# The order of products in the steps of a fused attention and Mish kernel

## Chip, cores and metric

One core of one Trainium2 chip. The metric is the device time of one execution in microseconds, the median of several runs.

## The reference

The input x is 1 x 2048 x 512. It is normalised over its last axis to xn. One branch is attention with 32 query heads of 16 and a single key and value head of 16; the other is a dense layer to 1792, Mish, and a dense layer back to 512. The sigmoid-weighted output of the second branch gates the first, and x is added.

```python
q = (xn @ wq)  as 32 heads of 16;  k = xn @ wk;  v = xn @ wv      # one k, one v for all heads
p = softmax(q k^T * 16**-0.5);  s = concat_heads(p v) @ wo
h = xn @ w1 + b1;  act = h * tanh(softplus(h));  g = silu(act @ w2)
out = x + s * g
```

All arrays are float32. The factors of 8 on the weights make the scores large enough that the softmax needs the row maximum.

## The kernel before

The four heads of a virtual group `v` (32 groups: four chunks of 512 queries times eight groups of heads) are treated together. A group takes 16 steps for its 16 blocks of 128 keys, so the main loop has 512 steps `s`. In each step PE issues:

- Four scores (`e_one`, L875): 128 keys by 512 queries from a contraction of 64 rows, into one of three banks `e`. ACT turns each into its exponential `pt` (L877).
- Four products for the row maxima of a later group (`m_one`, L895): 128 queries by 512 keys, into one of three banks `m`. DVE takes the maximum of each (L899). The maxima go back as extra rows of the queries, so that the exponential needs no bias of its own.
- A chunk of the dense work: the projections of q, the two dense layers and the output projection. A dense group accumulates 9 to 15 products of 128 rows in the only bank `x` (`xps`). `chunk_size` cuts a group of 12 into two chunks of six and one of 15 into chunks of eight and seven. Each product is split into two halves of 64 rows (`Mm.half`, L109): one step issues the lower halves of the chunk, the next the upper halves.
- The product of the exponentials of step s - 2 with the values (`pv`, L949).

Two products of 64 rows can run side by side on the two halves of PE's rows. `waves` writes out the order by hand. In step s the dense halves `xs` stand on side h = s % 2, followed by that side's products for maxima (the queue `b`). On the other side, 1 - h, stands the queue `a`: the four scores and n products for maxima, merged after the pattern `EM`; `m_sides` sets n, half the number of dense halves within limits given by `MLAG`. One round of the loop issues one dense half (or, when they are out, one product of `b`) and then one product of `a`; the last of `a` waits until the halves are out. With six halves n is 3 and `b` has one product, so a step has seven rounds; with seven halves, eight.

The two halves of one bank must not be written at once. `waves` therefore keeps a `relay`: the instruction on ACT or DVE that consumes a product issued after the last dense half of the step. The first dense half of the next step of the same group waits for it. When a group ends, `finish` calls its `post`, which empties the bank on ACT or DVE; for groups emptied by DVE, maxima of the last rounds are held back behind that (`HOLD`). After the products, ACT gets one or two pending jobs (`act_jobs`), and then comes `pv`.

Before the main loop a planner with costs and due times orders the normalisation, the first projections and the first maxima. The last 22 steps (`LEAD`) have no products for maxima, and the last groups of the dense work run unsplit after the loop. The engines' program orders are fixed when the kernel is built; on the chip only waits move them.

Of the kernel before, what the change touches and what calls it, by code (L numbers as in the profile page):

```python
# [41 lines left out]
STEP_US = 2.95  # L42
XMAX = 8
NPT = 14
EM = "MEMEMEME"
MLAG = 4
NHB = 3
NACT = 7
# [11 lines left out]
def m_need(v):  # L60

    return (40, 64)[v] if v < 2 else 32 * (v + 1)
# [53 lines left out]
def block_kernel(ctx: ExitStack, tc: tile.TileContext, x, wq, wk, wv, wo, w1, b1, w2, out):  # L116
# [348 lines left out]
    def begin():  # L465
        prepare()
        if qqueue and is_ready(qqueue[0]):
            g = qqueue.popleft()
        elif queue and is_ready(queue[0]):
            g = queue.popleft()  # L470
        else:
            n = next((n for n, g in enumerate(queue) if g.wo is None), None)
            if not n or not is_ready(queue[n]) or queue[n].m1 is None:
                return False
            g = queue[n]
            del queue[n]
        if g.start:
            g.start()
        if g.alloc:
            ps = g.alloc()  # L480
        else:
            ps = ps_x.tile([P, 512], F32, tag="x", name="xps")
        cur.update(g=g, n=0, ps=ps, chunk=[], relay=None)
        return True

    def finish():
        g = cur["g"]
        if cur["n"] < len(g.mms):
            return False
        for i in g.items:  # L490
            i.users -= 1
        cur["g"] = None
        evacs[0] += g.dve
        if lead:
            lead["post"](g, cur["ps"])
        else:
            g.post(cur["ps"])
            g.done = step[0]
        return True
# [14 lines left out]
    def chunk_size(n):  # L514
        return -(-n // -(-n // XMAX)) if n else 0

    def waves(h, em, new):

        if not cur["chunk"] and (not new or cur["g"] is None and not begin()):
            mms = []
        else:
            g = cur["g"]
            mms = cur["chunk"] or g.mms[cur["n"]:cur["n"] + chunk_size(len(g.mms) - cur["n"])]
        second = bool(cur["chunk"])
        k = len(mms)
        ms = em(k)
        a = deque(ms[1 - h])  # L530
        b = deque(ms[h])
        ps = cur["ps"]
        ends = second and cur["n"] + k == len(cur["g"].mms)
        xs = deque(mms)
        relay = None
        first = True
        done = False
        while a or b or xs:
            if xs:
                i = xs.popleft().half(ps, h)  # L540
                if first and cur["relay"] is not None:
                    tc.add_manual_dep(i.ins, cur["relay"].ins.name, mybir.DependencyInfo(
                        mybir.DependencyClass.Sync, mybir.DependencyReason.DATA), reason="other half of the bank")
                first = False
                if ends and cur["g"].dve and len(xs) == HOLD:
                    held[0] = []
                if not xs and ends:
                    cur["n"] += k
                    cur["chunk"] = []
                    finish()  # L550
                    done = True
                    for top in held[0] or ():
                        top()
                    held[0] = None
            elif b:
                b.popleft()()
            if len(a) > 1 or a and not xs:
                r = a.popleft()()
                if k and not xs and relay is None:
                    relay = r  # L560
        if k and not done:
            assert relay is not None
            cur["relay"] = relay
            if second:
                cur["n"] += k
                cur["chunk"] = []
            else:
                cur["chunk"] = mms
# [295 lines left out]
    def e_one(s, i):  # L864

        v, r = divmod(s, 16)
        if s < NS - LEAD:
            a, k, p = 1 - s % 2, r - r % 2 + i // 2, i % 2
        else:
            a, k, p = i % 2, r, i // 2  # L870
        q = qt_of[v]
        o = 64 * a
        ps, tag = (ps_m, "m") if NS - LEAD <= s and i in ((1, 3) if s < NS - 4 else (3,)) else (ps_e, "e")
        e = ps.tile([P, C], F32, tag=tag, name=f"e{s}_{i}")
        pe.matmul(e, ks[o:o + 64, P * k:P * (k + 1)], q[o:o + 64, p], start=True, stop=True)  # L875
        pt = sb.tile([P, C], F32, tag="pt", name=f"pt{s}_{i}", bufs=NPT)
        r = act.activation(pt, e, AF.Exp, scale=0.25)  # L877
        pt_of[16 * v + k, p, a] = pt
        return r
# [3 lines left out]
    def m_one(a):  # L883
        v, n = MSEQ[m_next[a]] if m_next[a] < 64 else divmod(m_next[a], 32)
        m_next[a] += 1
        if v not in mb_of:
            mb_of[v] = sb.tile([P, 4, 16], F32, tag="mb", name=f"mb{v}", bufs=2)
        q = qt_of[v]
        kb, j = divmod(n, 8)
        p, t = divmod(j, 4)  # L890
        o = 64 * a
        ps, tag = (ps_e, "e") if lead and 15 in xp_of and a else (ps_m, "m")
        m = ps.tile([P, C], F32, tag=tag, name=f"m{v}_{a}_{n}")
        o = slice(o, o + (HALF if v < len(qts) else 48))
        pe.matmul(m, q[o, p, P * t:P * (t + 1)], ks[o, C * kb:C * (kb + 1)], start=True, stop=True)  # L895
        z = 8 * a + 4 * p + t

        def top():
            return dve.reduce_max(out=mb_of[v][:, kb, z:z + 1], in_=m, axis=AX.X)  # L899
        if held[0] is None:  # L900
            return top()
        held[0].append(top)

    def m_sides(h, n):

        ahead = m_next[h] - m_next[1 - h]
        lo = max((4 - MLAG - ahead + 1) // 2, 4 - (32 * NU - m_next[1 - h]))
        hi = min((4 + MLAG - ahead) // 2, 32 * NU - m_next[h])
        return max(min(n, hi), lo)
# [116 lines left out]
    def due(t):  # L1026
        step[0] = t
        for k in sorted(k for k in timed if k <= t):
            for fn in timed.pop(k):
                fn()  # L1030
# [85 lines left out]
    for c0, c1 in ((0, 1), (1, 2), (2, 4)):  # L1116
# [4 lines left out]
        for c in range(c0, c1):  # L1121
            xs, his = [], []
# [29 lines left out]
            if c == 0:  # L1152
                qp = task("PE", 2.8, lambda: fill(12), xs)
                xs = [qp]
# [45 lines left out]
    while True:  # L1200
# [21 lines left out]
        s, e, k = min(opts, key=lambda o: o[0])  # L1222
# [36 lines left out]
        elif k == "J":  # L1259
            tag = next((g for g in ("wq", "ws", "wb") if arrived(g) and busy[0] + E0 < s + 0.5), None)  # L1260
            n = ran[0]
# [16 lines left out]
    while left:  # L1278
        k = next(k for k in left if all(d.end is not None for d in k.deps))
# [6 lines left out]
    for s in range(NS + 2000):  # L1286
        inm = s < NS - LEAD
        if inm or cur["chunk"]:
            assert s < NS
            due(s)  # L1290
            h = s % 2

            def em(k):
                n = m_sides(1 - h, k // 2) if inm else 0
                x = deque(lambda i=i: e_one(s, i) for i in range(4))
                y = deque(lambda: m_one(1 - h) for _ in range(n))
                r = [[], []]
                for op in EM:
                    if op == "M" and y:
                        r[1 - h].append(y.popleft())  # L1300
                    elif op == "E":
                        r[1 - h].append(x.popleft())
                r[h] = [lambda: m_one(h) for _ in range(4 - n if inm else 0)]
                return r

            if s >= 2 and (s - 1) % 16 == 0 and s > 1:
                gap[0] += 1
            waves(h, em, inm)
            act_jobs(1 + (len(jobs) > 2))
            due(s + 0.5)  # L1310
            if s >= 2:
                pv(s - 2)
                if (s - 1) % 16 == 0 and s > 1:
                    o_out((s - 17) // 16)
        else:
            due(s)
            if s < NS:
                for i in range(4):
                    e_one(s, i)
                fill(4)  # L1320
            act_jobs(2 if s < NS else 100)
            if s < NS + 2:
                pv(s - 2)
                if (s - 1) % 16 == 0:
                    o_out((s - 17) // 16)
            due(s + 0.5)
            if s >= NS:
                fill(16)
        step[0] = s
        if vdone[0] < 8 * NC and min(m_next) >= m_need(vdone[0]):  # L1330
            r = c_rows(vdone[0])
            rowq.extend([r[0], r[1], lambda r=r: (r[2](), r[3]())])
            vdone[0] += 1
        if rowq and not evacs[0]:
            rowq.popleft()()
        evacs[0] = 0
        pump()
        if s > NS + 1 and not queue and cur["g"] is None and not timed and not jobs:
            break
# [12 lines left out]
```

## Time and profile before

| What | Value |
|---|---|
| Median of 3 runs | 1616.48 us (1615.63 to 1619.14) |
| Span of the profiled execution, first to last instruction | 1612.9 us |
| PE busy | 1594.2 us, 99% |
| DVE busy | 1348.5 us, 84% |
| ACT busy | 1294.7 us, 80% |
| POOL busy | 620.8 us, 38% |
| Mean granted clock of PE | 0.999 |

The page gives the span of the profiled execution, and no time of its own beside it; the median of the runs is 3.6 us above that span. Engines: PE is the matrix engine, PEld its weight loads, DVE the vector engine, ACT the scalar engine, POOL the general one, SP the engine that issues the DMAs. In a row of the timeline the columns are the start, the duration, the engine, the line, the operation, the tile written and the tiles read, the shapes, and the number of instructions merged; behind that may stand the idle time before it and what ended it. In a row of the list of waits stand the waiting engine and tile, the one waited for, the total, the number of times and the longest.

### The profile page before, as it was taken

How to read it: one execution, taken by the hardware profiler on the slowest of the kernel's cores; microseconds unless marked ns; L12 is line 12 of the kernel's file. 1: busy time of each engine (PE TensorE's matmuls, PEld its weight loads, DVE VectorE, ACT ScalarE, POOL GpSimd, SP SyncE). 2: the span in 40 equal slices, each digit the busy share in tenths (PEclk: the TensorE clock that was granted, in tenths of full speed). 3: DMA queues.
4: the chain of work that ended last, by engine and by line, in shares of the span. 5: the costliest groups of instructions: out<-in, count | busy, mean ns of one | idle time of the engine just before them, and what ended most of it. 6: DMA issues, size and time to landing. Idle time of an engine off the chain costs nothing.

```text
span 1612.9 us, 31471 instructions
## 1 busy us (share of the span) xinstructions
PE 1594.2 (99%) x11615; PEld 851.9 (53%) x11615; DVE 1348.5 (84%) x2300; ACT 1294.7 (80%) x2490; POOL 620.8 (38%) x627
## 2 busy tenths in 40 slices
PE   8999999999999999999999999999999999999998
PEld 5455545555555555555555555555555555555534
DVE  8988888888988888888898988888889898888802
ACT  5478788788888778877988787797788878879885
POOL 3875176166265103421524133154153223315522
PEclk9999999999999999999999999999999999999999
DMA  5332133042231304212113321231241313022020
GB/s 161 145 115 64 41 122 111 15 148 83 70 114 52 109 23 153 70 31 91 52 27 111 92 75 26 91 119 38 67 135 34 113 57 96 23 73 78 21 86 26
DMA packets 72776, 127.30 MB, mean 79 GB/s; under 512 B 21488, under 2 KB 34288, under 8 KB 72112
## 3 DMA queue, kind: packets, MB, share of 16 engines
q1 hardware_dynamic: 72624, 125.30, 24.9%
q8 instruction: 92, 1.51, 0.4%
q14 instruction: 60, 0.49, 0.1%
HBM read 76.36 MB, written 27.26 MB: 64 GB/s over the span
## 4 chain that ended last, share of the span: by engine, by line
PE 95%; DVE 2%; ACT 1%; DMA 1%; issue 0%; POOL 0%; SPq 0%; DVEq 0%; ACTq 0%; POOLq 0%
PE xps L109 46%; PE pv L949 31%; PE m L895 8%; PE e L875 5%; PE xps L105 3%; DVE mb L899 1%; PE wop L105 1%; PE warm L1178 0%; PE kp L289 0%; ACT xin L194 0%; DMA xin<-in_dram 0%; DVE st L214 0%; DMA ws<-w 0%; DVE xin L240 0%; PE xp L250 0%
## 5 line engine op out<-in xcount | busy, mean ns | idle before, releaser
L899 DVE TENSOR_REDUCE mb<-m 128x1 f32<-128x512 f32 x2048 | 1272.8, 683 | 184.4 <-PE m L895 157.5
L877 ACT ACTIVATE pt<-e 128x512 f32<-128x512 f32 x2048 | 1068.4, 604 | 253.0 <-PE e L875 236.8
L895 PE MATMUL m<-ks,qt 48*128 48x512 f32 (+1 forms) x2048 | 837.4, 422 | 3.0 <-DVE mb L899 2.5
L875 PE MATMUL e<-qt,ks 64*128 64x512 f32 x2048 | 746.4, 410 | 0.0
L949 PE MATMUL pv<-pt,vaug 128*32 128x512 f32 x4096 | 545.3, 605 | 0.0
L895 PEld LDWEIGHTS m<-ks,qt 48*128 48x128 f32 (+1 forms) x2048 | 370.6, 185 | 67.2 <-DVE mb L899 35.2
L875 PEld LDWEIGHTS e<-qt,ks 64*128 64x128 f32 x2048 | 370.7, 186 | 26.3 <-ACT pt L877 19.6
L109 PE MATMUL xps<-xt,ws 64*128 64x512 f32 x1248 | 345.8, 410 | 0.4 <-POOL ws L153 0.2
L109 PEld LDWEIGHTS xps<-xt,ws 64*128 64x128 f32 x1248 | 215.2, 185 | 205.9 <-ACT pt L877 135.2
L109 PE MATMUL xps<-wbs,act 64*128 64x512 f32 x1158 | 312.9, 407 | 0.1
L109 PEld LDWEIGHTS xps<-wbs,act 64*128 64x128 f32 x1158 | 201.9, 185 | 166.8 <-ACT pt L877 101.5
L949 PEld LDWEIGHTS pv<-pt,vaug 128*32 128x32 f32 x4096 | 80.7, 108 | 141.9 <-issue 133.2
L163 POOL TENSOR_SCALAR t<-t 128x512 f32<-128x512 f32 x56 | 34.5, 616 | 278.4 <-ACT t L658 278.4
L153 POOL TENSOR_TENSOR hb<-hb,t 128x512 f32<-128x512 f32 x56 | 72.3, 1292 | 152.4 <-PE m L895 74.0
L109 PE MATMUL xps<-xt,wq 64*128 64x512 f32 x336 | 93.0, 409 | 0.0
L109 PEld LDWEIGHTS xps<-xt,wq 64*128 64x128 f32 x336 | 58.0, 185 | 55.4 <-ACT pt L877 35.2
L109 PE MATMUL xps<-wbs,ot_all 64*128 64x512 f32 x288 | 79.3, 407 | 0.0
L109 PEld LDWEIGHTS xps<-wbs,ot_all 64*128 64x128 f32 x288 | 49.5, 184 | 47.2 <-ACT pt L877 30.2
L153 POOL TENSOR_TENSOR hb<-hb,u 128x512 f32<-128x512 f32 x56 | 72.3, 1291 | 4.4
L153 POOL TENSOR_TENSOR u<-u,t 128x512 f32<-128x512 f32 x56 | 71.9, 1284 | 4.7
L153 POOL TENSOR_TENSOR act<-hb,act 128x512 fp32r<-128x512 f32 x55 | 70.9, 1289 | 4.6
L721 DVE TENSOR_TENSOR y<-xps,y 128x512 f32<-128x512 f32 x32 | 21.9, 683 | 58.0 <-PE xps L105 58.0
(116 smaller groups left out, 826.7 us busy)
## 6 DMA issues: line engine op xcount, KB each, us to landing
ws<-w SPq DMA_DIRECT2D x38, 512.0 KB
wbs<-w SPq DMA_DIRECT2D x36, 512.0 KB
qt<-qh SPq DMA_DIRECT2D x256, 32.0 KB
w<-ws SPq DMA_DIRECT2D x14, 512.0 KB
w<-wbs SPq DMA_DIRECT2D x14, 512.0 KB
wq<-wq SPq DMA_DIRECT2D x13, 512.0 KB
wbs<-wo SPq DMA_DIRECT2D x12, 512.0 KB
rawwb<-in_dram SPq DMA_DIRECT2D x20, 256.0 KB
```

Of the source, the lines that this page charges most:

```text
L105: self.pe.matmul(ps, self.lhs(), self.rhs(), start=(self.k == 0), stop=(self.k == self.tot - 1))
L109: i = self.pe.matmul(ps, self.lhs()[o], self.rhs()[o], start=(self.k == 0 and self.halves == 0), stop=(self.k == self.tot - 1 and self.hal ...
L153: eng.tensor_tensor(out=o, in0=a, in1=b, op=op)
L163: pool.tensor_scalar(o, o, lim, 0.0, op0=ALU.min, op1=ALU.max)
L721: dve.tensor_tensor(out=y, in0=ps, in1=y, op=ALU.add)
L875: pe.matmul(e, ks[o:o + 64, P * k:P * (k + 1)], q[o:o + 64, p], start=True, stop=True)
L877: r = act.activation(pt, e, AF.Exp, scale=0.25)
L895: pe.matmul(m, q[o, p, P * t:P * (t + 1)], ks[o, C * kb:C * (kb + 1)], start=True, stop=True)
L899: return dve.reduce_max(out=mb_of[v][:, kb, z:z + 1], in_=m, axis=AX.X)
L949: pe.matmul(o[32 * j:32 * j + 32], vaug[:, k], pt, start=(k == 0), stop=(k == 15))
```

## The change

In a step with fewer than eight dense halves, and some, in which n is 3, the side with the scores takes the pattern E M E M E M E in place of M E M E M E E. The relay becomes the consumer of the last product that is issued after the halves, in place of the first one.

```diff
-EM = "MEMEMEME"
+EM = ("MEMEMEME", "EMEMEME")
...
             if len(a) > 1 or a and not xs:
                 r = a.popleft()()
-                if k and not xs and relay is None:
+                if k and not xs:
                     relay = r
...
-                for op in EM:
+                for op in EM[0 < k < XMAX and n == 3]:
                     if op == "M" and y:
                         r[1 - h].append(y.popleft())
                     elif op == "E":
```

## The prediction

> **What bounds the kernel now.** I read the page first, then the list of waits, then the timeline of single steps, and last the stretches by window.
>
> ```profile
> span 1612.9 us, 31471 instructions
> PE 1594.2 (99%) x11615; PEld 851.9 (53%) x11615; DVE 1348.5 (84%) x2300; ACT 1294.7 (80%) x2490; POOL 620.8 (38%) x627
> ...
> PE 95%; DVE 2%; ACT 1%; DMA 1%; issue 0%; POOL 0%; SPq 0%; DVEq 0%; ACTq 0%; POOLq 0%
> ...
> L899 DVE TENSOR_REDUCE mb<-m 128x1 f32<-128x512 f32 x2048 | 1272.8, 683 | 184.4 <-PE m L895 157.5
> L877 ACT ACTIVATE pt<-e 128x512 f32<-128x512 f32 x2048 | 1068.4, 604 | 253.0 <-PE e L875 236.8
> ```
>
> PE carries 95% of the chain of waits. Its program order is fixed, so the time is the sum of its steps, and a wait inside a step is added directly. Two consumers empty its banks: a maximum takes DVE 683 ns, an exponential takes ACT 604 ns. Here is one undisturbed step with six dense halves (PE and weight loads in the timeline, then the first maximum and the first exponential by themselves):
>
> ```profile
> 808.94 0.16 PEld L949 LDWEIGHTS pv<-pt,vaug 128*32 128x32 f32 x8 [0.25 <-issue]
> ...
> 809.79 0.65 ACT L729 ACTIVATE e<-y 128x512 f32<-128x512 f32 x1
> 809.94 0.18 PEld L109 LDWEIGHTS xps<-wbs,act 64*128 64x128 f32 x1 [0.84 <-ACT pt L877]
> ...
> 809.94 0.50 PE L895 MATMUL m<-ks,qt 48*128 48x512 f32 x1
> ...
> 810.28 0.40 PE L875 MATMUL e<-qt,ks 64*128 64x512 f32 x1
> ...
> 810.51 1.89 DVE L899 TENSOR_REDUCE mb<-m 128x1 f32<-128x512 f32 x3 [0.37 <-PE m L895]
> ...
> 811.22 0.40 PE L875 MATMUL e<-qt,ks 64*128 64x512 f32 x1
> 811.26 0.18 PEld L895 LDWEIGHTS m<-ks,qt 48*128 48x128 f32 x1
> 811.37 0.18 PEld L875 LDWEIGHTS e<-qt,ks 64*128 64x128 f32 x1
> ...
> 811.79 0.16 PEld L949 LDWEIGHTS pv<-pt,vaug 128*32 128x32 f32 x8 [0.24 <-issue]
> ...
> 810.51 0.69 DVE L899 TENSOR_REDUCE mb<-m 128x1 f32<-128x512 f32 x1 [0.37 <-PE m L895]
> ...
> 810.72 0.60 ACT L877 ACTIVATE pt<-e 128x512 f32<-128x512 f32 x1 [0.28 <-PE e L875]
> ```
>
> The step is pv (808.94 to 809.94, 1.00 us) and then seven slots of two matmuls, one on each half of the rows (809.94 to 811.79, 1.85 us). The first slot takes 0.34 us (809.94 to 810.28), because its weight load is bare; the others take some 0.235 us ((811.22 - 810.28)/4). I call the products on the score side M1, E1, M2, E2, M3, E3, E4, with M4 on the other side in the seventh slot just ahead of E4. Both kinds have three banks, so M4 needs the bank of M1, and E4 that of E1. E1 comes a slot later than M1: its exponential ends at 811.32 and E4's load starts at 811.37, 0.05 us after. So E4 is the tight one, and when E1's exponential is late, pv is late by as much:
>
> ```profile
> 744.09 0.60 ACT L877 ACTIVATE pt<-e 128x512 f32<-128x512 f32 x1 [0.65 <-PE m L895]
> ...
> 744.74 0.18 PEld L875 LDWEIGHTS e<-qt,ks 64*128 64x128 f32 x1 [0.28 <-ACT pt L877]
> ...
> 745.17 0.16 PEld L949 LDWEIGHTS pv<-pt,vaug 128*32 128x32 f32 x8 [0.24 <-issue]
> ...
> PEld xps L109 <- ACT pt L877: 302.1, 360, 1.1
> PEld m L895 <- DVE mb L899: 35.2, 75, 0.8
> PEld xps L109 <- DVE y L721: 21.7, 25, 0.9
> PEld e L875 <- ACT pt L877: 19.6, 33, 0.8
> PEld xps L109 <- issue: 12.6, 15, 0.8
> ...
> L949 PEld LDWEIGHTS pv<-pt,vaug x568: 106/108/109, 348.7 to 550.9; 128*32 128x32 f32 x190
> L949 PEld LDWEIGHTS pv<-pt,vaug x480: 106/108/109, 794.5 to 966.0; 128*32 128x32 f32 x160
> 346.00:552.00 206.00, 206.00 (x1572) 110.95 (x1566) 184.12 (x314) 176.44 (x340) 102.81 (x104) 1.00 0.29 91
> ```
>
> The exponential ends at 744.69, the load follows at 744.74, and pv 0.43 us later. The longest row of the list, 302.1 us for the relay, is a trap: 302.1/360 is 0.84 us, and the 15 times with no wait at all ("issue") also make 12.6/15 = 0.84 us. That is the time in which pv's matmuls occupy the array. The relay costs next to nothing now. In a long stretch of six-half steps the 568 loads of pv are 71 steps (8 each), so one step takes (550.9 - 348.7)/70 = 2.889 us; a second stretch of such steps gives (966.0 - 794.5)/59 = 2.907. I take 2.90, against 2.85 for the undisturbed step: about 0.05 us a step is lost to late exponentials, all that the reordering could give back.
>
> **How many steps change.** The halves by their rows:
>
> ```profile
> L109 PE MATMUL xps<-xt,ws 64*128 64x512 f32 x1248 | 345.8, 410 | 0.4 <-POOL ws L153 0.2
> L109 PE MATMUL xps<-wbs,act 64*128 64x512 f32 x1158 | 312.9, 407 | 0.1
> L109 PE MATMUL xps<-xt,wq 64*128 64x512 f32 x336 | 93.0, 409 | 0.0
> ...
> L109 PE MATMUL xps<-wbs,ot_all 64*128 64x512 f32 x288 | 79.3, 407 | 0.0
> ```
>
> A group of 12 products is 24 halves in four steps of six. 1248, 336 and 288 are 52 + 14 + 12 = 78 such groups. The 1158 are 29 groups of 15 products (8 + 8 + 7 + 7 halves; the program has 32, three of them fall in the unsplit end) and (1158 - 870)/24 = 12 groups of 12. So 90 x 4 = 360 steps of six, 58 of seven, 58 of eight. With six or seven the score side gets k//2 = 3 maxima unless the lead limit MLAG makes it two, as it does in a few steps after an idle one; I take 355 steps of six.
>
> **The new order.** The side becomes E1, M1, E2, M2, E3, M3, E4, with M4 still just ahead of E4 in the seventh slot. No instruction is added or removed, and no DMA or Pool work moves. E1 is now six slots ahead of E4, so E4's wait is gone. But M1 moves from slot one to slot two, five slots ahead of M4. The same tight distance passes from the exponential (0.60 us) to the longer maximum (0.69 us), and what is next late is M4's load. Behind it in PE's queue stand E4 and pv, and behind those the next step.
>
> M1 starts at 0.34 us in the step. From a matmul of slot two to its consumer the trace has 0.44 us (810.28 to 810.72) and, in the step below, 0.49 us (801.64 to 802.13). For DVE in this slot there is no row. In slot one it began 0.57 us after the matmul, with a bare weight load of about 0.1 in that, so I take ACT's two values as bounds. A value under 0.40 is not open, since that is the matmul's own row. Then the maximum, 0.69. What follows a late bank of M is in the trace too, in a step where DVE was held up by the output stage's product with y (L153):
>
> ```profile
> 801.64 0.39 PE L875 MATMUL e<-qt,ks 64*128 64x512 f32 x1
> ...
> 802.13 1.09 ACT L877 ACTIVATE pt<-e 128x512 f32<-128x512 f32 x2
> ...
> 520.61 0.68 DVE L899 TENSOR_REDUCE mb<-m 128x1 f32<-128x512 f32 x1
> ...
> 521.34 0.18 PEld L895 LDWEIGHTS m<-ks,qt 48*128 48x128 f32 x1 [0.22 <-DVE mb L899]
> 521.35 0.18 PEld L875 LDWEIGHTS e<-qt,ks 64*128 64x128 f32 x1
> 521.78 0.16 PEld L949 LDWEIGHTS pv<-pt,vaug 128*32 128x32 f32 x8 [0.25 <-issue]
> ...
> L721 DVE TENSOR_TENSOR y<-xps,y 128x512 f32<-128x512 f32 x32 | 21.9, 683 | 58.0 <-PE xps L105 58.0
> ...
> L153 DVE TENSOR_TENSOR y<-xps,y 128x512 f32<-128x512 f32 x12 | 8.2, 684 | 0.0
> ```
>
> M1's maximum ended at 521.29, M4's load came 0.05 later, E4's load 0.01 after that, pv 0.43 after that. So the new step is 1.00 (pv) + 0.34 + 0.44 to 0.49 + 0.69 + 0.05 + 0.01 + 0.43 = 2.96 to 3.01 us, middle 2.985; against 2.90 that is +0.06 to +0.11, middle 0.085. Times 355: **+21 to +39 us, middle +30**.
>
> The one soft link is the distance from M4's load to E4's: 0.11 us when nothing waits (811.26 to 811.37), 0.01 when M4 was late. I take 0.01, the row nearest to the new case; 0.11 in every step would add 0.10 x 355 = 35 us more. The Trainium skill, "TensorE: Matmul & The Clock Gate", section "Step-by-step: what each phase is for", says that weight loads are pulled ahead of matmuls in flight when their row groups don't conflict, which would make this distance zero and the sum 0.01 x 355 = 4 us smaller; the late row agrees with it, the undisturbed one does not show it.
>
> **DVE's other work.** In the new step the maxima follow each other at the 0.60 us of now ((1.89 - 0.69)/2), M1 starting at about 0.80, so M4's ends near 0.80 + 1.81 + 0.68 = 3.29, 0.30 into the next step; M1 of that step comes at 0.80. An operation on y (0.68, some 0.60 in a row of DVE work) fills more than the 0.50 us left and makes M1 late by 0.1. There are 32 + 12 of them (L721, L153), 44 x 0.1, and I take 3 us, since some fall on seven-half steps. Bounds: 0, and 44 x 0.18 = 8 us if DVE is free only at 0.98.
>
> **The relay.** With six halves, seven products on the score side leave one after the last half: the relay was E3 and becomes E4. Its waiter is the first half of the next step, with the whole PE queue behind it. E4's load is now near 1.54 in the step; the product is there some 0.1 + 0.49 later, at 2.13, the exponential ends at 2.73, and the next first half is not due before 2.98. pv covers it with 0.25 us to spare. Without that cover it would cost up to 0.6 us. An ACT job (0.65, as at 809.79) from the step before delays E1 but is caught up before E4. I take 1 us in all; bounds 0, and for some 270 steps that use a relay 0.03 each, 8 us.
>
> **Seven and eight halves.** With seven, M4 stands in slot eight, alone and six slots after M1 in the new order, the distance that costs nothing now; the relay is E4 before and after. With eight nothing changes. I cost both at nothing: their cover is the eighth slot, 0.235 us, and without it the 58 steps of seven would add 58 x 0.1 = 6 us.
>
> **The sum.** 30 + 3 + 1 = +34. It is made on a span of 1612.9 us; the median of the runs, 1616.48, is 3.6 above it, and I add the difference to the median: **1650 us**. Ends: the low one 1616 + 21 = 1637; the high one 1616 + 39 + 8 + 8 = 1671.
>
> **Rivals.**
> The reordering pays (faster): E4 no longer waits, and M4's wait is hidden. Then the step falls to the undisturbed 2.85 or a little under, -0.05 x 355 = -18 us: 1598. It decides at M1's maximum ending by 1.38 in the step, which E1's exponential does now; it would have to start by 0.69, only 0.35 after its matmul's start. The late exponentials and the 19.6 us of waits for them speak for it, the 0.40 us matmul row against it. 6%.
> The relay becomes the bound: if an ACT job regularly stands between E3 and E4, 0.65 us in the exponential's way, E4 ends at 3.4 and each of 270 steps pays 0.4: 108 us more, 1762. The jobs are issued after all four exponentials, which speaks against it. 5%.
> The change does nothing: if the lead limit gave two maxima in most steps, the old order would stand for them, 1616. The split of M between the sides alternates evenly, so it should give three. 2%.
> PE's clock: the extra wait could let the granted clock fall, and the 0.235 us slots would double; 1.85 more in 355 steps is +657 us, 2273. The granted clock is 1.00 in the whole stretch above, although M4 waited for its bank at 521.34 in it. The Trainium skill, "TensorE: Matmul & The Clock Gate", section "A second HAM failure mode: psum-queue depth-cycling", tells of a kernel that idled briefly between bank rounds and lost its clock; this trace shows no such drop. 1%.
>
> **Numbers.** The forecast of a wait moved to M4 has 85%. A measurement of this kernel can tell about 0.2%, 3.2 us. Faster is the first rival, 6%; same is the third and 1% for a chance cancelling of the two waits, 3%; slower is the forecast, the relay and the clock, 91%. The range 1630 to 1671 runs from the low end, with 7 us off it for a DVE that starts 0.02 sooner after slot two than ACT's quickest row, to the high end; it leaves out the rivals and the soft link's 35 us.
>
> **What would show it.** Right: M4's load carries a wait for DVE in nearly all six-half steps, the row "m <- DVE mb" grows from 75 times to some 350, "e <- ACT pt" shrinks, ACT starts its first exponential before DVE its first maximum, and the 70 steps of the long stretch average 2.96 to 3.01 us. Relay: first half more than 1.00 us after pv begins. Wrong: M4's load at 1.32 in the step as now, or pv starting 1.85 or less after the first half.

## The result and the profile after

The changed kernel takes 1642.13 us (median of 4 runs, 1641.57 to 1642.40), the kernel before 1616.06 (4 runs, the three above and one more). The ratio is 1.016, 95% interval 1.0146 to 1.0174: 26 us slower. The forecast was 1650 in a range of 1630 to 1671.

The page of the changed kernel, with the rows that answer to those shown of before:

```profile
span 1639.8 us, 31653 instructions
...
PE 1621.6 (99%) x11615; PEld 795.5 (49%) x11615; DVE 1348.0 (82%) x2300; ACT 1312.3 (80%) x2490; POOL 620.6 (38%) x627
...
PE 96%; DVE 2%; ACT 1%; issue 0%; DMA 0%; SPq 0%; DVEq 0%; ACTq 0%
PE xps L109 41%; PE pv L949 31%; PE m L895 14%; PE e L875 6%; PE xps L105 3%; DVE mb L899 1%; PE wop L105 1%; PE warm L1178 0%; PE kp L289 0%; ACT xin L194 0%; DVE st L214 0%; DMA xin<-in_dram 0%; DVE xin L240 0%; PE xp L250 0%; DVE ks L153 0%
...
L895 PEld LDWEIGHTS m<-ks,qt 48*128 48x128 f32 (+1 forms) x2048 | 372.0, 186 | 162.9 <-DVE mb L899 144.7
```

The span grew by 26.9 us. The counted work is the same to the instruction on every engine (the 182 instructions more in the span's line only wait for semaphores, all on ACT), and PE still makes nearly all of the chain; what changed is how long it stands in front of m. The list of waits says where:

```profile
PEld xps L109 <- ACT pt L877: 291.8, 348, 0.9
PEld m L895 <- DVE mb L899: 144.7, 408, 0.8
PEld e L875 <- ACT pt L877: 18.6, 29, 0.8
```

The loads for maxima waited for DVE 75 times before and do so 408 times now; 354 of these are M4's in steps of six halves, 19 before. The list leaves out idle times of less than 0.15 us, so M4 had shorter waits before as well: its load stood at 1.316 us in the step, 0.05 after the end of M1's maximum at 1.263 (medians), but E4's load came later still, at 1.48. The row of the relay is still pv's own time (291.8/348 = 0.84 us). The list counts idle time of the loading side, during which PE may still stream, so the 110 us that its middle row gained are not the loss: the lost time is read from the steps. Here is one of six halves, the weight loads in the timeline:

```profile
370.00 0.18 PEld L109 LDWEIGHTS xps<-xt,wq 64*128 64x128 f32 x1 [0.84 <-ACT pt L877]
370.00 0.18 PEld L875 LDWEIGHTS e<-qt,ks 64*128 64x128 f32 x1
...
371.55 0.18 PEld L895 LDWEIGHTS m<-ks,qt 48*128 48x128 f32 x1 [0.30 <-DVE mb L899]
371.55 0.18 PEld L875 LDWEIGHTS e<-qt,ks 64*128 64x128 f32 x1
371.97 0.16 PEld L949 LDWEIGHTS pv<-pt,vaug 128*32 128x32 f32 x8 [0.24 <-issue]
```

And the first maximum and the first exponential of that step, and the loads of pv over a long stretch of such steps:

```profile
370.80 0.69 DVE L899 TENSOR_REDUCE mb<-m 128x1 f32<-128x512 f32 x1 [0.49 <-PE m L895]
...
370.54 0.60 ACT L877 ACTIVATE pt<-e 128x512 f32<-128x512 f32 x1 [0.28 <-PE e L875]
```

```profile
L949 PEld LDWEIGHTS pv<-pt,vaug x576: 106/108/109, 348.1 to 559.4; 128*32 128x32 f32 x192
```

E1's exponential ends at 371.14, long before E4's slot; its wait is gone. M1's maximum runs from 370.80 to 371.49, M4's load follows at 371.55, E4's directly behind it, and pv 0.42 after that, 1.97 us into the step instead of the 1.85 of the undisturbed one (over all 359 steps of six halves the median is 1.977 against 1.905 before). The stretch has 72 steps, (559.4 - 348.1)/71 = 2.976 us each, against 2.889 before.

### The profile page after: what moved, and what is told of

It reads as the page before. It is cut to its first block, busy times and chain, and to the rows that moved or that the text cites. A ratio compares the mean times of both kernels' runs of the same rounds, so it can differ in the third digit from the quotient of the medians.

```text
span 1639.8 us, 31653 instructions
## 1 busy us (share of the span) xinstructions
PE 1621.6 (99%) x11615; PEld 795.5 (49%) x11615; DVE 1348.0 (82%) x2300; ACT 1312.3 (80%) x2490; POOL 620.6 (38%) x627
## 4 chain that ended last, share of the span: by engine, by line
PE 96%; DVE 2%; ACT 1%; issue 0%; DMA 0%; SPq 0%; DVEq 0%; ACTq 0%
PE xps L109 41%; PE pv L949 31%; PE m L895 14%; PE e L875 6%; PE xps L105 3%; DVE mb L899 1%; PE wop L105 1%; PE warm L1178 0%; PE kp L289 0%; ACT xin L194 0%; DVE st L214 0%; DMA xin<-in_dram 0%; DVE xin L240 0%; PE xp L250 0%; DVE ks L153 0%
## 5 line engine op out<-in xcount | busy, mean ns | idle before, releaser
L877 ACT ACTIVATE pt<-e 128x512 f32<-128x512 f32 x2048 | 1087.8, 601 | 258.3 <-PE e L875 240.5
L875 PE MATMUL e<-qt,ks 64*128 64x512 f32 x2048 | 864.7, 436 | 0.0
L895 PE MATMUL m<-ks,qt 48*128 48x512 f32 (+1 forms) x2048 | 788.1, 418 | 4.2 <-DVE mb L899 3.8
```

## The experiments

All ratios are to runs of the kernel before on the same chip. The first set splits the change in two.

**The order without the relay, and the relay without the order.**

```diff
 order_only (from the changed kernel)
-                if k and not xs:
+                if k and not xs and relay is None:
                     relay = r
 relay_only (from the kernel before)
-                if k and not xs and relay is None:
+                if k and not xs:
                     relay = r
```

> The new order alone: the relay is again the consumer of the first product after the last half (with six halves, now M3's maximum). Theory (M4 waits for the bank that M1's maximum frees): all of the loss stays, 1642 us, the step of six halves 2.97 to 2.98 us. Rival (the later relay makes the loss): back to 1616 us, step 2.90.

> The new relay alone, in the old order (with six halves, E4's exponential in place of E3's). Theory: in the profile before, E4's exponential ends 2.07 us after E1's begins, which is just when pv lets the next half start, so 0 to 0.03 us a step for some 270 steps: 1616 to 1624 us, and the first half starts up to some 0.05 later than 1.00 after pv in a part of the steps. Rival (the later relay makes the loss): 1642 us.

Measured: order_only 1635.56 us, ratio 1.0121 (1.0106 to 1.0136); relay_only 1628.48 us, ratio 1.0077 (1.0062 to 1.0092). Both theories missed something: the order alone costs some 18 us and not all of the loss, and the relay alone costs 11 or 12, above the bound that I had set. In relay_only the timeline shows the relay bind: E4's exponential is the last of the four, pv starts, and the first half of the next step comes late.

```profile
384.32 2.06 ACT L877 ACTIVATE pt<-e 128x512 f32<-128x512 f32 x4 [0.21 <-PE e L875]
385.41 0.16 PEld L949 LDWEIGHTS pv<-pt,vaug 128*32 128x32 f32 x8 [0.25 <-issue]
...
386.44 0.18 PEld L109 LDWEIGHTS xps<-wbs,act 64*128 64x128 f32 x1 [0.88 <-ACT pt L877]
```

```profile
L949 PEld LDWEIGHTS pv<-pt,vaug x576: 106/108/109, 347.4 to 555.6; 128*32 128x32 f32 x192
```

E4's exponential ends at 386.38 and the first half starts 0.06 later, 1.03 us after pv began, where 1.00 is pv's own time. Over the 359 steps of six halves, the first half after such a pv came more than 0.015 us later than 0.996 in 270 of them, against 6 before, 14 us together against 0.5. In the old order E4's exponential ends as pv does, and the 0.05 us from ACT to PE, which I had left out of that expectation, then lies bare. The mean step of the stretch is (555.6 - 347.4)/71 = 2.932.

The two parts don't add: against the median of 1617.1 us of the kernel before on that chip they are 18.5 + 11.4, or 30 us, and the change costs 26. In the changed kernel the relay no longer makes a first half late (1 of 359). The new order starts the exponentials some 0.2 us sooner (E1's at 0.54 in the step above) and pv starts 0.07 later, so E4's exponential ends 0.26 us before pv's own time is over (median), where relay_only leaves 0.003. Yet the new order with the old relay is 6.6 us faster than with the new one. The stretch of order_only and one of its steps show how:

```profile
371.31 0.18 PEld L109 LDWEIGHTS xps<-xt,wq 64*128 64x128 f32 x1 [0.84 <-DVE mb L899]
...
371.65 0.39 PE L895 MATMUL m<-ks,qt 48*128 48x512 f32 x1
...
372.08 1.29 DVE L899 TENSOR_REDUCE mb<-m 128x1 f32<-128x512 f32 x2 [0.47 <-PE m L895]
```

```profile
L949 PEld LDWEIGHTS pv<-pt,vaug x576: 106/108/109, 349.5 to 559.5; 128*32 128x32 f32 x192
```

M1's maximum starts 0.77 us into the step, 0.03 sooner than the 0.80 of the changed kernel, and the mean step is (559.5 - 349.5)/71 = 2.958 against 2.976. I come back to this below.

**A dose on M1's maximum, and the same dose elsewhere.** A dose is a known amount by which one duration alone is changed, to see whether the time follows.

```diff
-    def m_one(a):
+    def m_one(a, w=C):
...
-            return dve.reduce_max(out=mb_of[v][:, kb, z:z + 1], in_=m, axis=AX.X)
+            return dve.reduce_max(out=mb_of[v][:, kb, z:z + 1], in_=m[:, 0:w], axis=AX.X)
...
-                y = deque(lambda: m_one(1 - h) for _ in range(n))
+                cut = 0 < k < XMAX and n == 3
+                y = deque(lambda w=W if cut and j == J else C: m_one(1 - h, w) for j in range(n))
```

Here J is 0 for M1 and 1 for M2, and W the columns that are read. These kernels leave columns out of one maximum, and in all four the scale of the exponentials is 0.02 in place of 0.25 (not shown here); after_m2_256, which has both, takes as long as the changed kernel, so neither makes a difference by itself.

> The changed kernel, but in steps of six and seven halves the first maximum (M1) reads 448 of its 512 columns; the exponentials' scale is 0.02 in place of 0.25, so that they stay finite. A dose: the maximum gets shorter by 64/512 of its 0.6 or so, 0.07 us. Theory: pv starts 0.07 sooner in 355 steps, -24 us: 1618 us. Rival (the order itself is slower, by a score in the bare first slot or by ACT): 1642 us.

> The same with M1's maximum over 256 of the 512 columns, 0.27 us shorter. Theory: M4's bank is free before M4's slot comes, and E1's exponential now has six slots, so nothing waits in the step and it falls to its slots: 2.84 to 2.85 us against 2.975, -0.13 x 355 = -46 us: 1596 us, faster than before. Rival (the order itself is slower): 1642 us.

> The changed kernel with the second maximum of the step (M2) over 256 of the 512 columns, and the exponentials' scale 0.02. Theory: M4 takes M1's bank, not M2's, so nothing changes: 1640 to 1642 us. Rival (DVE has too much work in a step, whichever maximum it is): about as fast as with M1 shortened, 1596 us.

> The kernel before with M1's maximum over 256 of the 512 columns in steps of six and seven halves, and the exponentials' scale 0.02. Theory: before, E4's wait for E1's exponential was the late one and M4's was not, so nothing changes: 1614 to 1617 us. Rival (shorter work on DVE speeds the step up in any order): 1596 us.

Measured: after_m1_448 1620.10 us, ratio 1.0027 (1.0016 to 1.0038); after_m1_256 1597.62, ratio 0.9886 (0.9869 to 0.9902); after_m2_256 1642.03, ratio 1.0166 (1.015 to 1.0182); before_m1_256 1615.49, ratio 0.9998 (0.9987 to 1.0008). All four went as the theory had them and against the rivals. The rows of after_m1_256 and of after_m2_256:

```profile
PEld m L895 <- DVE mb L899: 32.5, 53, 0.8
```

```profile
L949 PEld LDWEIGHTS pv<-pt,vaug x576: 106/108/109, 344.5 to 546.5; 128*32 128x32 f32 x192
```

```profile
L949 PEld LDWEIGHTS pv<-pt,vaug x576: 106/108/109, 349.0 to 560.2; 128*32 128x32 f32 x192
```

With M1's maximum halved, the waits of m fall from 408 to 53 and the step to (546.5 - 344.5)/71 = 2.845; with M2's halved it is (560.2 - 349.0)/71 = 2.975, as in the changed kernel. So the loss is neither DVE's amount of work nor the order as such, but the time until M1's bank is free. In before_m1_256 M4's load moves from 1.316 to 1.272 us in the step and pv stays at 1.906, since E4 comes later: M4's short wait in the old order cost nothing. This also prices both waits: a step in which neither product waits costs 2.845, so the kernel before paid 0.05 a step for E1 and the changed one pays 0.13 for M1.

**Where E4 stands, and the steps of seven.**

```diff
 after_e4_first
-            elif b:
+            elif b and not (k == 6 and len(a) == 1):
                 b.popleft()()
 seven_only
-                for op in EM[0 < k < XMAX and n == 3]:
+                for op in EM[k == 7 and n == 3]:
```

> The changed kernel, but in the seventh slot of steps of six halves E4 is issued ahead of M4, so that E4 does not stand behind M4 in PE's queue. Theory: pv still stands behind M4, which waits for M1's bank: 1640 to 1643 us, E4's load at 1.3 to 1.45 in the step, M4's at 1.55 as before. Rival (the loss is E4 standing behind M4): back to 1600 to 1616 us.

> The new order in steps of seven halves alone, with the new relay in all steps. Theory: the 58 steps of seven have an eighth slot that covers M1, so the order costs nothing there; what differs from before is the relay of the six-half steps. So the time of relay_only, within 3 us. Rival (seven-half steps lose 0.1 us as well): 6 us more than relay_only.

Measured: after_e4_first 1641.86 us, ratio 1.0161 (1.0146 to 1.0177); seven_only 1630.29, ratio 1.0091 (1.0074 to 1.0108). The timeline of after_e4_first, its first half at 369.92:

```profile
371.20 0.19 PEld L875 LDWEIGHTS e<-qt,ks 64*128 64x128 f32 x1
371.46 0.18 PEld L895 LDWEIGHTS m<-ks,qt 48*128 48x128 f32 x1
371.89 0.16 PEld L949 LDWEIGHTS pv<-pt,vaug 128*32 128x32 f32 x8 [0.25 <-issue]
```

E4's load moved to 1.28 us in the step, just under the 1.3 to 1.45 expected, and M4's stayed at 1.54; pv is held by M4 alone. And seven_only stands with relay_only (2 us apart, their intervals overlap), and the traces say the same: the mean step of seven halves takes 3.054 us in the kernel before, 3.050 in the changed one, 3.055 in relay_only and 3.054 in seven_only. The new order costs nothing there.

**The 6.6 us between the two relays.** The traces list for each instruction the semaphores that it waits for and raises. First half and second half are here the first two dense halves of a step; the second is issued just ahead of M1's product. In the changed kernel the first half waits for ACT, so the wait for DVE that M1's bank needs stands on M1's own weight load; the second half then raises PE's semaphore by itself, just ahead of M1's product. In order_only the first half waits for DVE already, M1's load mostly has no wait, and the second half mostly raises nothing: M1's product raises for both at once. To tell this from the relay itself, the first half was made to wait for both consumers:

```diff
 both_relays (from the changed kernel)
-                    tc.add_manual_dep(i.ins, cur["relay"].ins.name, ...
+                    for top in cur["relay"]:
+                        tc.add_manual_dep(i.ins, top.ins.name, ...
...
                 if k and not xs:
-                    relay = r
+                    relay = (relay or []) + [r]
```

> The changed kernel, whose first half waits for both relays (with six halves M3's maximum on DVE and E4's exponential on ACT). In the runs so far the new order with the old relay was 6.6 us faster than with the new one, although the first half starts 0.996 us after pv in both; there the first half waits for DVE, the second half of the step then has no wait of its own and raises no semaphore, and M1's maximum starts 0.776 us into the step in place of 0.801. Theory (the wait for M1's bank moves to the second half, whose semaphore increment stands just ahead of M1's): with DVE's wait back on the first half, M1's maximum starts at 0.776 again, 1635 to 1637 us. Rival (waiting for ACT's relay costs the 6.6 us itself): 1642 us.

Measured: 1638.62 us, ratio 1.0146 (1.0132 to 1.016), between the two, with an interval that overlaps both neighbours' (1.0106 to 1.0136 for order_only, 1.0146 to 1.0174 for the change). The mean step of six halves is clearer: 2.964 us, against 2.959 in order_only and 2.976 in the changed kernel. The wait stands on M1's load, and not on the second half as the expectation has it; the raise on the second half is as expected. In 221 steps of both_relays the first half waits for ACT, the second half raises nothing, and M1's maximum starts at 0.776 us in the step (median); in 72 steps the second half raises the semaphore, and it starts at 0.80. The same two values appear in order_only (255 and 73 steps), and the upper one in 326 of the 359 steps of the changed kernel. In two steps of order_only and two of both_relays the second half raises though M1's load doesn't wait, and the maximum starts at 0.80 there too, so it is not the wait. The 0.025 us at M1's start is thus shown to go with the increment ahead of it, and not with the relay's engine. The Trainium skill, "TensorE: Matmul & The Clock Gate", section "The cost: per-tile semaphore tail", says of small matmuls packed side by side as tiles that, when each increments a semaphore, the increments are made one after another, some 26 ns each; the 25 ns here agree.

In the other steps M1's maximum is later, and two causes stand in the trace: in 24 DVE was still at work on the maximum before, as in 24 of the changed kernel; in 30, against one in the changed kernel, E1's product starts 0.1 late and M1's with it 0.07. There three instructions of PE that only wait for a semaphore stand ahead of E1's load, some 0.11 to 0.125 us apart: the one that the second wait on the first half has added, and two for E1, the last of which starts no sooner than the first half does.

**A faster version.** In the kernel before, E1's exponential started 0.05 later after its matmul in many steps than in the others (0.49 us against 0.44), though ACT was idle. A one-column instruction on ACT was put at the end of the step:

```diff
 before_small_exp (from the kernel before)
+    small = cp.tile([P, 1], F32, name="small")
...
+            n0 = ran[0]
             act_jobs(1 + (len(jobs) > 2))
+            if inm and ran[0] == n0:
+                act.activation(small, one, AF.Exp)
 before_small_copy: AF.Copy in place of AF.Exp
 before_small_exp_all: if inm alone, so in every step
```

> The kernel before with one exponential of a single column on ACT at the end of each step in which ACT had no pending job. A trial of a faster version: E1's exponential started 0.44 us after its matmul in most steps in which ACT had run an exponential for a job, and 0.49 to 0.50 in most in which its last work was E4 itself. If short idle ACT makes it late, pv starts up to 0.05 sooner in some 100 to 160 steps: 1608 to 1612 us. Rival (the lateness has another cause): 1616 to 1618 us.

> As before_small_exp, with a copy of one column in place of the exponential. In the profile of before_small_exp the first exponential of a step starts 0.446 us after its matmul behind the small one, and 0.486 behind E4 in the kernel before; behind logarithms and copies it was late in the kernel before too. If any short work on ACT ahead of the wait helps: 1609 us, 0.996 of before. If it must be an exponential: 1616 us, 1.00 of before, and E1's exponential starts 0.48 to 0.50 after its matmul.

> The small exponential at the end of every step, also behind ACT's jobs. Some 135 steps of six halves have a logarithm, a copy or another job last, late by 0.04 in about half of them: 0.02 x 135 = 3 us less than before_small_exp, 0.994 of before, if ACT has room for some 0.2 us more in those steps; 0.996 to 1.0 if the longer work of ACT makes E1 late instead.

Measured: 1608.98 us, ratio 0.9962 (0.995 to 0.9975); with the copy 1607.32, 0.9958 (0.9945 to 0.997); in every step 1606.16, 0.9948 (0.9934 to 0.9961). Rows of before_small_exp, the groups and the stretch of pv:

```profile
L1313 ACT ACTIVATE small<-one 128x1 f32<-128x1 f32 x275 | 62.0, 225 | 0.0
```

```profile
L949 PEld LDWEIGHTS pv<-pt,vaug x576: 106/108/109, 346.8 to 551.0; 128*32 128x32 f32 x192
```

ACT does 62 us more work and the kernel is some 6 us faster: the mean step of the stretch is (551.0 - 346.8)/71 = 2.876, over all 359 steps it is 2.879 against 2.899 before, and E1's exponential starts 0.455 us after its matmul in place of 0.475. It needs no exponential; a copy does as well. The interval with one in every step overlaps the one of before_small_exp, so what the extra ones are worth is not shown. Why a short instruction ahead of the wait makes ACT start sooner was not settled.

## Why the prediction was right, point by point

- **The tight bank.** Right. The wait of five slots passed from E4 to M4. The dose of 64 columns took 22 us off and that of 256 took 44.5, the same dose on M2 or in the old order nothing. One sign named ahead told little: the row of e went only from 33 to 29, and 20 of these are in the last steps, which have no dense halves, in both kernels; in steps of six halves E4 has 12 and 5.
- **The size of a step.** 2.96 to 3.01 was forecast, 2.976 measured. Over all 359 steps of six halves the mean went from 2.899 to 2.976, which is 27.9 us of the span's 26.9; the other steps and the time ahead of the loop gave 1.0 back. The middle, 30, was 2 us too high. DVE took up M1 0.46 us after its matmul, in the middle of ACT's two rows, 0.44 and 0.49 (the next point accounts for the excess). That ACT's rows bounded it was in part luck: DVE has two values of its own here, 0.46 and 0.434, by the increment ahead, and ACT itself took up E1 in the new order 0.54 to 0.60 after its matmul.
- **The soft link.** M4's and E4's loads stand at the same 371.55 (medians of all steps 1.547 and 1.550). The value from the late row was right to 0.007 us, or 2.5 us in all, and the Trainium skill's rule on pulled-ahead loads, cited there, agrees as far as this goes. The 0.11 that the prediction reads as "when nothing waits" was a wait itself, E4's for E1's exponential, which had ended 0.05 before; with neither waiting (after_m1_256) the loads stand at 1.280 and 1.285.
- **DVE's other work.** Mis-sized: 3 us were taken for work on y. Of the 29 steps of six halves that follow such work, M1's maximum started at 0.82 to 0.83 in 24, up to 0.03 late, which makes under 1 us. I let DVE's overhang run to the full length of its last maximum, 0.68, where the next one follows after 0.60.
- **The relay.** E4's exponential ends at 2.71 in the step and leaves 0.26 us (medians), where 2.73 and 0.25 were forecast, and the 1 us that I took came out as none. But the step saw only the wait. That the relay's engine decides on which instruction the next wait stands, and so where a semaphore is raised, it did not see; this moved M1 by 0.025 us and is the 6.6 us between order_only and the change. It was inside the measured 0.46 and so inside the range that the two rows had left open. In the old order the same relay costs 11 or 12 us.
- **Seven and eight halves.** Right: the mean step of seven went from 3.054 to 3.050, of eight from 3.109 to 3.105.
- **The rivals.** The price of the fast one, 1598, is what after_m1_256 gives, 1597.6; its condition, M1's maximum ending by 1.38, does not hold at full width, where it ends at 1.49. The price of the relay as the bound has a slip: 108 us on 1650 is 1758, not 1762. PE's clock stayed at 0.999.

## What to carry to other kernels

When two kinds of products share a step and each has a ring of banks, give the longest distance to the consumer with the longest latency: here matmul to free bank is 1.1 us for the exponential and 1.2 us for the maximum, and the change cost 0.08 us in each of 359 steps. Work out, for each ring, when the oldest bank is free against when its next user's slot comes, and swap only if the engine that gains the slack is slower than the one that loses it. A wait that looks long in a list may be another instruction's time; compare it with the same gap where nothing was waited for. Ask, too, whether that gap is itself a short wait that the list leaves out.

## What the runs showed of the hardware

A semaphore raised by a matmul just ahead goes with a start of the next matmul's consumer that is 0.025 us later (DVE, M1's maximum at 0.802 in place of 0.776 us in the step), which in the some 250 steps in which the two kernels differ is 6 us here. Instructions of PE that only wait for a semaphore follow each other 0.11 to 0.125 us apart, and three of them ahead of E1's load made its product 0.1 us late in 30 steps of both_relays. And ACT took up a product 0.02 us sooner on average when a one-column instruction of 0.225 us stood ahead of the wait, with which the kernel before was 0.4% faster; why is not known.
